# Three buffers for the queries' parts, one bank apart, square sums side by side, and the first block's keys in two halves, in a transformer block's opening stage

## The chip, the cores and the metric

The kernel runs on one core of one Trainium2 chip, as one launch. Its time is the device time of one execution in microseconds (us). A core has a matrix engine (TensorE, PE below), a vector engine (VectorE, DVE), an activation engine (ScalarE, ACT), a general engine (GpSimd, POOL), a sequencer that mostly issues DMAs (SyncE, SP), and 16 DMA engines between the device memory and the on-chip memory. Each engine has a queue of its own and works it off in order; waits between engines go by semaphores. Products of PE land in PSUM, which has eight banks of 128 rows by 512 fp32 values.

## The reference

One pre-norm transformer block: attention with 32 query heads of 16 and one shared key and value head, then a gated feed-forward part. Everything is fp32; S = 2048 tokens, D = 512, F = 1792.

```python
q = (layernorm(x) @ wq).reshape(B, S, 32, 16).transpose(0, 2, 1, 3)
k, v = layernorm(x) @ wk, layernorm(x) @ wv
p = softmax(einsum("bhqd,bkd->bhqk", q, k) * 16 ** -0.5)
h = x + einsum("bhqk,bkd->bhqd", p, v).transpose(0, 2, 1, 3).reshape(B, S, 512) @ wo
out = h + (gelu(layernorm(h) @ w_gate) * (layernorm(h) @ w_up)) @ w_down
```

## The kernel before, in words

The tokens are cut into four blocks of 512 (b = 0 to 3), a block into four tiles of 128 (t = 0 to 15 over all blocks), D into four chunks of 128 (c or d). An fp32 product is made of three products of fp32r parts, high x high, high x low and low x high; every operand is split by a cast (`hi`) and a subtraction (`lo`).

**The opening (`prologue`).** For every tile t the program loads x, takes its statistics on DVE and POOL, normalizes it on ACT (`xn`), turns it on PE (`pt`, four transposes into one PSUM bank), and splits it into `xT_hi` (ACT) and `xT_lo` (DVE). Turn t issues the work of several tiles: PE gets the transposes of tile t, then one chunk of the previous block's keys (`project_k`, tile `pk`, three products of 512 tokens), then one chunk of the first queries (`project_q`, tile `pq`). `idle` is a bank for transposes whose result nobody reads; they stand between the first turns to keep PE running. `wk_rep` repeats the key's 16 columns, so that one product gives several copies of k and, in spare rows, v. The keys' square sums (`norm_k`, tile `pkn`, weights `ones`) give the largest square norm `k2m`.

**Queries (`project_q`).** A query chunk (b, c) is 128 rows, that is eight heads. Its product `pq` is cast to `qh`, and `ql` is what is left; both come from pools of two buffers (tags `qh` and `ql`). For three chunks, `HURRY = ((0, 3), (1, 0), (1, 1))`, `pq` is first copied to SBUF (`pq_raw`: by ACT for block 0, by DVE for block 1), so that its bank is free early. `qs` is the square of `qh` in bf16. SP writes `qh`, `ql` and `qh` again to `q_d` in device memory, from where a group of four heads is loaded as `qg` for the scores; a buffer of `qh` or `ql` is free again when these writes have landed. When the four chunks of a block are done, a product with the 0/1 matrix `sel` sums the squares of each head's 16 rows (`pqn`, 32 rows for 32 heads; the four chunks add up in the same rows, each with its own 32 columns of `sel`). DVE copies it to `qn` and takes the maximum over the tokens (`q2`); POOL works out two numbers per head in four small steps (`mm`, from `q2` and `k2m`), DVE makes `m` from them, a bound on the scores that goes to `q_d` as one more row of the query. In block 0 chunk 0 goes first (`q_first`, urgent) with its own `pqn`, `mm` and `m`, so that the first scores can start; chunks 1 to 3 follow (`q_rest`).

**Attention (`run`).** Scores `s` (PE) go through ACT's exponential to `p`, five buffers; `weigh` multiplies `p` with v into `acc` (one bank, four groups of 32 rows). A list of moves written by hand (`OPENING`, `PERIOD`) weaves scores (s), sums (v) and pieces of later blocks' queries (p) through the first block, which ends near 312 us of the span; the order of PE, ACT, POOL, and there also of DVE and SP, is the order in which the program issues. All through the first block POOL splits the weights of the feed-forward part and writes them back (`part_weights`); the four steps of `mm` stand between in its queue. `evacuate` copies a finished `acc` to `oT` on DVE. Later blocks weave the feed-forward products into the attention.

In the opening PSUM's eight banks are one pool, from which `psum1` takes the next free one. `check_bound` writes the product of the largest `q2` and `k2m` to `b_d`, from which a flag is made that a safe path hangs on.

Of the kernel before, what the change touches and what calls it, by code (L numbers as in the profile page):

```python
# [19 lines left out]
P = 128  # L20
# [8 lines left out]
FIRST_Q = 1  # L29

HURRY = ((0, 3), (1, 0), (1, 1))

OPENING = "ssspssps"

# [23 lines left out]
def kernel(  # L58
# [12 lines left out]
    nc = tc.nc  # L71
# [35 lines left out]
    nc.vector.memset(power[:, 0:1], -0.5)  # L107
    nc.vector.memset(power[:, 1:2], 0.5)

    q2 = const.tile([H, NB + 1], F32, name="q2")  # L110
# [47 lines left out]
    def run(outer, first):  # L158
# [25 lines left out]
        if first:  # L184
            eb = early.enter_context(tc.tile_pool(name="early", bufs=1))

            xT = {
                b: [eb.tile([P, DC, T], F32R, name=f"xT_{w}_{b}") for w in ("hi", "lo")]
                for b in range(1, NB)
            }  # L190
            wq_hi = [eb.tile([P, DC, P], F32R, name=f"wq_hi_{c}") for c in range(DC)]
            wq_lo = [eb.tile([P, DC, P], F32R, name=f"wq_lo_{c}") for c in range(DC)]
            sel = eb.tile([P, DC, H], BF16, name="sel")
            k2m = eb.tile([H, T // 32 + 1], F32, name="k2m")[:, :1]


        def project_q(b, cs, eng, col):
            tsl = slice(b * T, (b + 1) * T)
            xT_hi, xT_lo = xT[b]
            urgent = b == 0 and cs[0] == 0  # L200
            qss = []
            for c in cs:
                pq = psum1(f"pq_{b}_{c}")
                n = 0
                for d in range(DC):
                    for wt, xt in ((wq_hi, xT_hi), (wq_hi, xT_lo), (wq_lo, xT_hi)):
                        nc.tensor.matmul(  # L207
                            pq, wt[c][:, d, :], xt[:, d, :],
                            start=(n == 0), stop=(n == 3 * DC - 1),
                        )  # L210
                        n += 1
                    if urgent or d < DC - 1:
                        yield 3

                raw = None
                if (b, c) in HURRY:
                    raw = eb.tile([P, T], F32, tag="vT", bufs=3, name=f"pq_raw_{b}_{c}")
                    if b == 0:
                        nc.scalar.activation(raw, pq, AF.Copy)
                    else:  # L220
                        nc.vector.tensor_copy(raw, pq)
# [12 lines left out]
                qss.append(qs)  # L234
                for r0, part in ((0, qh), (DH, ql), (2 * DH, qh)):
                    nc.sync.dma_start(
                        q_d[c * HC : (c + 1) * HC, r0 : r0 + DH, tsl].bitcast(F32),
                        part.bitcast(F32),
                    )
                if raw is None or b == 0:  # L240
                    yield 4 if b > 0 and c == DC - 1 else 3

            pn = psum1(f"pqn_{b}_{cs[0]}")[:H, :]
            for i, c in enumerate(cs):
                nc.tensor.matmul(
                    pn, sel[:, c, :], qss[i], start=(i == 0), stop=(i == len(cs) - 1)
                )
            qn = eb.tile([H, T], F32, tag="qn", bufs=1, name=f"qn_{b}_{cs[0]}")
            nc.vector.tensor_copy(qn, pn)
            nc.vector.tensor_reduce(q2[:, col : col + 1], qn, axis=AX.X, op=ALU.max)  # L250
            if urgent:
                yield 2
            mm = eb.tile([H, 3], F32, tag="mm", bufs=2, name=f"mm_{b}_{cs[0]}")
            nc.gpsimd.tensor_scalar(
                mm[:, 0:1], q2[:, col : col + 1], k2m, 1e-30, op0=ALU.mult, op1=ALU.add
            )
            nc.gpsimd.tensor_tensor(mm[:, 1:2], mm[:, 0:1], power[:H, 0:1], op=ALU.pow)
# [3 lines left out]
            nc.gpsimd.tensor_scalar(  # L261
                mm[:, 1:2], mm[:, 1:2], k2m, 0.5, op0=ALU.mult, op1=ALU.mult
            )
            m = eb.tile([H, T], F32R, tag="m", bufs=2, name=f"m_{b}_{cs[0]}")
# [7 lines left out]
            nc.vector.tensor_scalar(m, qn, mm[:, 1:2], mm[:, 2:3], op0=ALU.mult, op1=ALU.add)  # L272
            hs = slice(cs[0] * HC, (cs[-1] + 1) * HC)
            nc.sync.dma_start(q_d[hs, 3 * DH, tsl].bitcast(F32), m[hs].bitcast(F32))
            yield 0

        ms = {}
# [897 lines left out]
    def prologue(psum1, xT, wq_hi, wq_lo, sel, k2m, q_first, q_rest, advance, first_q, first_bound, eb):  # L1175
        with ExitStack() as pro:
# [25 lines left out]
            def repeat_k():  # L1202
# [8 lines left out]
                )  # L1211


            nc.gpsimd.memset(sel, 1.0)
            nc.gpsimd.affine_select(
                out=sel, in_=sel, compare_op=ALU.is_ge, fill=0.0, base=0,
                pattern=[[P, DC], [-DH, H]], channel_multiplier=1,
            )
            nc.gpsimd.affine_select(
                out=sel, in_=sel, compare_op=ALU.is_ge, fill=0.0, base=DH - 1,  # L1220
                pattern=[[-P, DC], [DH, H]], channel_multiplier=-1,
            )

            bias = sb.tile([P, 1], F32, name="bias")
# [5 lines left out]
            ones = sb.tile([DH, H], BF16, name="ones")  # L1230
            nc.vector.memset(ones, 1.0)
            k2 = sb.tile([H, NB], F32, name="k2")
            nc.vector.memset(v_sb, 1.0)

            zero = sb.tile([H, S], F32R, name="zero")
# [31 lines left out]
                    nc.vector.tensor_tensor, lo, pt, hi.bitcast(F32), op=ALU.subtract  # L1267
                )

            def project_k(b, c):  # L1270
                xT_hi, xT_lo = xT[b]
                if c == 0:
                    pks[b] = psum1(f"pk_{b}")
                for n, (wt, xt) in enumerate(((wk_hi, xT_hi), (wk_hi, xT_lo), (wk_lo, xT_hi))):
                    nc.tensor.matmul(  # L1275
                        pks[b], wt[:, c, :], xt[:, c, :],
                        start=(c == 0 and n == 0), stop=(c == DC - 1 and n == 2),
                    )

# [3 lines left out]
                return ks  # L1283

            def norm_k(b, ks):
                pn = psum1(f"pkn_{b}")[:H, :]
                nc.tensor.matmul(pn, ones, ks, start=True, stop=True)
                return pn

# [52 lines left out]
            for t in range(NT):  # L1342
# [86 lines left out]
    b_d = dram.tile([1, H], F32, name="b_d")  # L1429

    def check_bound(sb, k2m):
        q2m = sb.tile([H, 1], F32, name="q2m")
        nc.vector.tensor_reduce(q2m, q2, axis=AX.X, op=ALU.max)
        nc.vector.tensor_tensor(q2m, q2m, k2m, op=ALU.mult)
        nc.sync.dma_start(b_d.rearrange("o h -> h o"), q2m)

    def bound_flag(step):
        if step == 0:
# [74 lines left out]
```

## Time and profile before

| | us |
|---|---|
| median of 3 runs (lowest to highest) | 1410.09 (1409.43 to 1411.04) |
| the profiled execution | 1410.79 |
| its span, first to last instruction | 1409.1 |
| PE busy | 1390.7 (99%) |
| ACT busy | 1034.0 (73%) |
| DVE busy | 629.8 (45%) |
| POOL busy | 231.5 (16%) |

All times of the profile count from the span's start. A busy PE is one with a matmul in flight; matmuls overlap, so a row of several has a total, and the distance between starts is the price of one. A matmul on fp32 values that are not fp32r stands as two instructions. The opening lasts about 47 us, the first block of attention until about 312 us, and the last block's feed-forward part begins near 1200 us.

### The profile page before, as it was taken

The page shows a single profiled execution, that of the slowest core. Times are in us where ns is not written, and L with a number is a line of the kernel's source. Part 1 is how long each engine was busy: PE and PEld are TensorE (multiplying, and loading weights), DVE is VectorE, ACT ScalarE, POOL GpSimd, SP SyncE. Part 2 cuts the span into 40 slices and gives each one's busy share as a digit, 9 for nine tenths or more (in the row PEclk, how much of TensorE's full clock was granted, in tenths as well). Part 3 has the DMA queues.
Part 4 walks back from the last instruction along what each step waited for, and adds up shares of the span by engine and source line. Part 5 has one row for each costly group of instructions (what it writes and reads, how often), then busy time and mean ns, then how long its engine had stood idle before and what let it go on. Part 6 is the DMA issues. An engine that isn't in the chain of part 4 may idle for free.

```text
span 1409.1 us, 25259 instructions
## 1 busy us (share of the span) xinstructions
PE 1390.7 (99%) x10435; PEld 760.2 (54%) x10435; DVE 629.8 (45%) x1022; ACT 1034.0 (73%) x1155; POOL 231.5 (16%) x335
## 2 busy tenths in 40 slices
PE   9999999999999999999999999999999999999998
PEld 7433333325455555555555555545555555558886
DVE  7311231214364454454354453435264453546665
ACT  7699999997877777777777777787778777762000
POOL 7575777731000000000000000000000000011000
PEclk9999999999999999999999999999999999999999
DMA  4565776745222333311432333310433332233552
GB/s 161 159 189 177 231 235 217 240 144 189 69 91 83 117 106 113 102 65 57 156 104 87 119 116 102 103 65 28 149 102 102 117 102 101 92 120 114 193 204 96
DMA packets 66707, 180.32 MB, mean 128 GB/s; under 512 B 9596, under 2 KB 9596, under 8 KB 66552
## 3 DMA queue, kind: packets, MB, share of 16 engines
q1 hardware_dynamic: 55120, 143.15, 30.7%
q0 software_dynamic: 10208, 35.26, 7.6%
q8 instruction: 84, 1.38, 0.4%
q10 hardware_dynamic: 1256, 0.20, 0.1%
q14 instruction: 39, 0.32, 0.1%
HBM read 130.87 MB, written 47.45 MB: 127 GB/s over the span
## 4 chain that ended last, share of the span: by engine, by line
PE 95%; ACT 2%; DMA 1%; DVE 1%; issue 1%; POOL 0%; SPq 0%; ACTq 0%; DVEq 0%
PE acc L362 33%; PE s L354 20%; PE pu L781 9%; PE pg L781 8%; PE pd L781 8%; PE pq L207 3%; PE pd L811 3%; PE pg L811 3%; PE pu L811 3%; PE pp L781 2%; ACT p L358 1%; PE pk L1275 1%; PE pp L883 1%; PE pd_rest L823 1%; DMA x<-in_A_x_dram 0%
## 5 line engine op out<-in xcount | busy, mean ns | idle before, releaser
L358 ACT ACTIVATE p<-s 128x1024 f32<-128x1024 f32 x1024 | 960.0, 1037 | 233.3 <-PE s L354 230.5
L362 PE MATMUL acc<-p,v_sb 128*32 128x512 f32 x4096 | 491.6, 600 | 0.0
L354 PE MATMUL s<-qg,kaug 50*128 50x512 f32 x1984 | 387.6, 426 | 4.1 <-ACT p L358 4.1
L354 PEld LDWEIGHTS s<-qg,kaug 50*128 50x128 f32 x1984 | 169.5, 184 | 282.5 <-ACT p L358 123.6
L362 PEld LDWEIGHTS acc<-p,v_sb 128*32 128x32 f32 x4096 | 108.9, 109 | 232.8 <-issue 219.9
L781 PE MATMUL pg<-x2h,w 64*128 64x512 f32 x672 | 175.2, 392 | 0.0
L781 PE MATMUL pu<-x2h,w 64*128 64x512 f32 x672 | 174.0, 392 | 0.0
L781 PE MATMUL pd<-w,gh 64*128 64x512 f32 x624 | 124.9, 393 | 1.4 <-DVE h L711 1.4
L711 DVE TENSOR_TENSOR h<-h,pd 128x512 f32<-128x512 f32 x80 | 54.4, 687 | 148.5 <-PE pd L781 148.5
L137 POOL TENSOR_SCALAR rstd<-mv 128x1 f32<-128x1 f32 x16 | 3.5, 221 | 674.0 <-DVE mv L135 673.8
L781 PEld LDWEIGHTS pg<-x2h,w 64*128 64x128 f32 x672 | 95.5, 186 | 11.3
L781 PEld LDWEIGHTS pu<-x2h,w 64*128 64x128 f32 x672 | 95.2, 186 | 11.5
L781 PE MATMUL pg<-x2l,w 64*128 64x512 f32 x336 | 100.1, 392 | 0.0
L781 PE MATMUL pu<-x2l,w 64*128 64x512 f32 x336 | 99.6, 392 | 0.0
L781 PEld LDWEIGHTS pd<-w,gh 64*128 64x128 f32 x624 | 69.6, 186 | 12.5 <-DVE h L711 2.7
L939 ACT ACTIVATE ga<-ga 128x512 f32<-128x512 f32 x14 | 8.8, 632 | 88.5 <-DVE ga L936 88.5
L781 PE MATMUL pd<-w,gl 64*128 64x512 f32 x312 | 72.7, 392 | 0.0
L375 DVE COPY oT<-acc 128x512 f32<-128x512 f32 x32 | 22.1, 690 | 112.0 <-PE acc L362 111.9
L648 DVE TENSOR_TENSOR g<-g,pg 128x512 f32<-128x512 f32 x42 | 28.8, 685 | 90.8 <-PE pg L781 90.8
L398 DVE RECIPROCAL oc<-oc 128x128 f32<-128x128 f32 x64 | 56.6, 922 | 20.2 <-DMA oc<-acc_d 16.4
L644 DVE COPY g<-pg 128x512 f32<-128x512 f32 x42 | 29.1, 692 | 72.1 <-PE pg L781 72.1
L648 DVE TENSOR_TENSOR u<-u,pu 128x512 f32<-128x512 f32 x42 | 28.8, 686 | 68.7 <-PE pu L781 68.7
(258 smaller groups left out, 1481.6 us busy)
## 6 DMA issues: line engine op xcount, KB each, us to landing
w<-w_d SPq DMA_DIRECT2D x126, 512.0 KB
w<-w_d SPq DMA_DIRECT2D x21, 1024.0 KB
qg<-q_d SPq DMA_DIRECT2D x62, 200.0 KB
q_d<-qh SPq DMA_DIRECT2D x32, 256.0 KB
acc_d<-oT SPq DMA_DIRECT2D x31, 256.0 KB
oc<-acc_d SPq DMA_DIRECT2D x124, 64.0 KB
w_d<-w_0b POOLq DMA_DIRECT2D x14, 512.0 KB, 5.0
w_d<-w_1b POOLq DMA_DIRECT2D x14, 512.0 KB, 3.3
```

The lines of the kernel that those rows point to most:

```text
L207: nc.tensor.matmul(pq, wt[c][:, d, :], xt[:, d, :], start=(n == 0), stop=(n == 3 * DC - 1),)
L354: nc.tensor.matmul(s[:, a, :], kaug[rows, kc * P : (kc + 1) * P], qg[rows, u, :], start=True, stop=True,)
L358: nc.scalar.activation(p[:, 2 * u : 2 * u + 2, :], s, AF.Exp, scale=SCALE)
L362: nc.tensor.matmul(acc[32 * j : 32 * j + 32, :], v_sb[:, kc, :], p[:, j, :], start=(kc == 0), stop=(kc == KC - 1), skip_group_check=True,)
L375: nc.vector.tensor_copy(oT, acc)
L398: nc.vector.reciprocal(oc[:, 1, sl], oc[:, 1, sl])
L644: nc.vector.tensor_copy(half, bank)
L648: nc.vector.tensor_tensor(half, half, bank, op=ALU.add)
L711: nc.vector.tensor_tensor(hs[b, t], hs[b, t], bank, op=ALU.add)
L781: nc.tensor.matmul(bank, lhsT[r], rhs[r], start=(k == 0), stop=(k == n - 1), skip_group_check=True,)
L811: nc.tensor.matmul(bank, lhsT, rhs, start=(i == 0), stop=(i == len(ts) - 1))
L823: nc.tensor.matmul(bank, lhsT, rhs, start=(i == 0), stop=(i == len(ts) - 1))
```

## The change

- `qh` and `ql` have three buffers each.
- `idle`, `pq_0_0` and `pq_0_3` share one bank of their own (`APART`, tag `apart`); all other tiles of the opening take turns in the seven that are left.
- `sel` has one set of 32 columns, eight heads in rows 0 to 7 of 32. Each chunk's square sum goes to its own 32 rows of `pqn`, so the four products of a block write side by side instead of adding up. `qn`, `mm`, `m`, `q2`, `k2`, `k2m` have up to 128 rows accordingly, `ones` has 128 columns, `m` has one buffer, and its rows are written to `q_d` by one DMA per chunk; `b_d` is filled by four.
- Block 0's keys are made in two halves of 256 tokens: the first half, all four chunks, in the turn of tile 4, the second in the turns of tiles 5 and 6, two chunks each. In all blocks high x high is followed by `wk_lo` x high and then `wk_hi` x low.

```diff
+APART = "idle", "pq_0_0", "pq_0_3"
...
         def psum1(name):
+            if name in APART:
+                return ps.tile([P, T], F32, tag="apart", bufs=1, name=name)
...
-                qh = eb.tile([P, T], F32R, tag="qh", bufs=2, name=f"qh_{b}_{c}")
-                ql = eb.tile([P, T], F32R, tag="ql", bufs=2, name=f"ql_{b}_{c}")
+                qh = eb.tile([P, T], F32R, tag="qh", bufs=3, name=f"qh_{b}_{c}")
+                ql = eb.tile([P, T], F32R, tag="ql", bufs=3, name=f"ql_{b}_{c}")
...
-            pn = psum1(f"pqn_{b}_{cs[0]}")[:H, :]
-            for i, c in enumerate(cs):
+            rows = slice(0, 32 * len(cs))
+            pn = psum1(f"pqn_{b}_{cs[0]}")[rows]
+            for i in range(len(cs)):
                 nc.tensor.matmul(
-                    pn, sel[:, c, :], qss[i], start=(i == 0), stop=(i == len(cs) - 1)
-                )
+                    pn[32 * i : 32 * i + 32, :], sel, qss[i], start=True, stop=True,
+                    skip_group_check=True,
+                )
...
-            hs = slice(cs[0] * HC, (cs[-1] + 1) * HC)
-            nc.sync.dma_start(q_d[hs, 3 * DH, tsl].bitcast(F32), m[hs].bitcast(F32))
+            for i, c in enumerate(cs):
+                nc.sync.dma_start(
+                    q_d[c * HC : (c + 1) * HC, 3 * DH, tsl].bitcast(F32),
+                    m[32 * i : 32 * i + HC].bitcast(F32),
+                )
...
-            width = 8
+            width = 7
...
-            def project_k(b, c):
+            def project_k(b, c, sl=slice(0, T)):
...
-                for n, (wt, xt) in enumerate(((wk_hi, xT_hi), (wk_hi, xT_lo), (wk_lo, xT_hi))):
+                for n, (wt, xt) in enumerate(((wk_hi, xT_hi), (wk_lo, xT_hi), (wk_hi, xT_lo))):
                     nc.tensor.matmul(
-                        pks[b], wt[:, c, :], xt[:, c, :],
+                        pks[b][:, sl], wt[:, c, :], xt[:, c, sl],
...
+            K_HALVES = {0: (0, range(DC)), 1: (1, range(2)), 2: (1, range(2, DC))}
...
-                    if 0 <= step < DC:
+                    if b == 0 and step in K_HALVES:
+                        half, cs = K_HALVES[step]
+                        for c in cs:
+                            project_k(0, c, slice(half * T // 2, (half + 1) * T // 2))
+                    elif b > 0 and 0 <= step < DC:
                         project_k(b, step)
```

PE's queue in the turn of tile 4, before (the first number behind a name is its buffer's; `pk_360` is block 0's keys, `pt_374` is tile 5):

```order
L1332 MATMUL idle<-ident 128x128 x3
L1275 MATMUL pk_360<-xT_hi_113,wk_hi 128x512
L1275 MATMUL pk_360<-xT_lo_114,wk_hi 128x512
L1275 MATMUL pk_360<-xT_hi_113,wk_lo 128x512
L1261 MATMUL pt_374<-ident,xn_336 128x128 x4
```

And now (`pk_361` is block 0's keys):

```order
L1343 MATMUL idle<-ident 128x128 x3
L1285 MATMUL pk_361<-xT_hi_113,wk_hi 128x256
L1285 MATMUL pk_361<-xT_hi_113,wk_lo 128x256
L1285 MATMUL pk_361<-xT_lo_114,wk_hi 128x256
L1285 MATMUL pk_361<-xT_hi_113,wk_hi 128x256
```

The three products of 256 tokens stand there four times, twelve in all, ahead of tile 5's transposes; the product with `xT_lo` has moved from second to third.

PE's queue in the turn of tile 7, before (`pt_425` is tile 7, `pt_449` tile 8, `pq_0_385` the first queries):

```order
L1261 MATMUL pt_425<-ident,xn_380 128x128 x4
L1275 MATMUL pk_360<-xT_hi_113,wk_hi 128x512
L1275 MATMUL pk_360<-xT_lo_114,wk_hi 128x512
L1275 MATMUL pk_360<-xT_hi_113,wk_lo 128x512
L207 MATMUL pq_0_385<-xT_hi_113,wq_hi_94 128x512
L207 MATMUL pq_0_385<-xT_lo_114,wq_hi_94 128x512
L207 MATMUL pq_0_385<-xT_hi_113,wq_lo_98 128x512
L1261 MATMUL pt_449<-ident,xn_405 128x128 x4
```

And now (`pt_441` and `pt_462` are tiles 7 and 8):

```order
L1271 MATMUL pt_441<-ident,xn_390 128x128 x4
L211 MATMUL pq_0_398<-xT_hi_113,wq_hi_94 128x512
L211 MATMUL pq_0_398<-xT_lo_114,wq_hi_94 128x512
L211 MATMUL pq_0_398<-xT_hi_113,wq_lo_98 128x512
L1271 MATMUL pt_462<-ident,xn_418 128x128 x4
```

The keys' three products are gone from this turn.

PE's queue where the first scores start, with the semaphores that each row waits for, before (`s_0_781` and `s_1_785` are the first two score tiles):

```order
L207 MATMUL pq_3_746<-xT_hi_113,wq_lo_101 128x512
L354 MATMUL s_0_781<-qg_first,kaug 128x512 [waits DMAHW1_49,DMAHW6_49,DVE_49,Activation_49]
L354 MATMUL s_0_781<-qg_first,kaug 128x512 [waits DMAHW7_49,DMAHW2_49,DMAHW0_49]
L354 MATMUL s_1_785<-qg_first,kaug 128x512 [waits DMAHW3_49]
L354 MATMUL s_1_785<-qg_first,kaug 128x512 [waits DMAHW2_49]
```

And now (`s_0_794` and `s_1_798` are the same two):

```order
L211 MATMUL pq_3_759<-xT_hi_113,wq_lo_101 128x512
L363 MATMUL s_0_794<-qg_first,kaug 128x512 [waits DMAHW1_49,DMAHW6_49,DVE_49,Activation_49]
L363 MATMUL s_0_794<-qg_first,kaug 128x512 [waits DMAHW7_49,DMAHW2_49,DMAHW0_49]
L363 MATMUL s_1_798<-qg_first,kaug 128x512 [waits DMAHW3_49]
L363 MATMUL s_1_798<-qg_first,kaug 128x512 [waits DMAHW2_49]
```

Nothing has moved here: the first score product waits for DVE and ACT as before. DVE's, ACT's and SP's other instructions stand in the same order as before; only widths differ, and `m`'s writes are three or four in a row.

More of the change, by code (lines that the diff above doesn't have):

```diff
@@ L108 @@
     nc.vector.memset(power[:, 1:2], 0.5)
-    q2 = const.tile([H, NB + 1], F32, name="q2")
+    q2 = const.tile([P, NB + 1], F32, name="q2")
     flag = const.tile([1, 1], I32, name="flag")
@@ L192, in run @@
             wq_lo = [eb.tile([P, DC, P], F32R, name=f"wq_lo_{c}") for c in range(DC)]
-            sel = eb.tile([P, DC, H], BF16, name="sel")
-            k2m = eb.tile([H, T // 32 + 1], F32, name="k2m")[:, :1]
+            sel = eb.tile([P, DC * H], BF16, name="sel")[:, :H]
+            k2m = eb.tile([P, T // 32 + 1], F32, name="k2m")[:, :1]
         def project_q(b, cs, eng, col):
@@ L241, in project_q @@
                     yield 4 if b > 0 and c == DC - 1 else 3
-            pn = psum1(f"pqn_{b}_{cs[0]}")[:H, :]
-            for i, c in enumerate(cs):
+            rows = slice(0, 32 * len(cs))
+            pn = psum1(f"pqn_{b}_{cs[0]}")[rows]
+            for i in range(len(cs)):
                 nc.tensor.matmul(
-                    pn, sel[:, c, :], qss[i], start=(i == 0), stop=(i == len(cs) - 1)
-                )
-            qn = eb.tile([H, T], F32, tag="qn", bufs=1, name=f"qn_{b}_{cs[0]}")
+                    pn[32 * i : 32 * i + 32, :], sel, qss[i], start=True, stop=True,
+                    skip_group_check=True,
+                )
+            qn = eb.tile([P, T], F32, tag="qn", bufs=1, name=f"qn_{b}_{cs[0]}")[rows]
+            top = q2[rows, col : col + 1]
             nc.vector.tensor_copy(qn, pn)
-            nc.vector.tensor_reduce(q2[:, col : col + 1], qn, axis=AX.X, op=ALU.max)
+            nc.vector.tensor_reduce(top, qn, axis=AX.X, op=ALU.max)
             if urgent:
                 yield 2
-            mm = eb.tile([H, 3], F32, tag="mm", bufs=2, name=f"mm_{b}_{cs[0]}")
-            nc.gpsimd.tensor_scalar(
-                mm[:, 0:1], q2[:, col : col + 1], k2m, 1e-30, op0=ALU.mult, op1=ALU.add
-            )
-            nc.gpsimd.tensor_tensor(mm[:, 1:2], mm[:, 0:1], power[:H, 0:1], op=ALU.pow)
+            mm = eb.tile([P, 3], F32, tag="mm", bufs=2, name=f"mm_{b}_{cs[0]}")[rows]
+            km = k2m[rows]
+            nc.gpsimd.tensor_scalar(mm[:, 0:1], top, km, 1e-30, op0=ALU.mult, op1=ALU.add)
+            nc.gpsimd.tensor_tensor(mm[:, 1:2], mm[:, 0:1], power[rows, 0:1], op=ALU.pow)
             nc.gpsimd.tensor_scalar(
@@ L261, in project_q @@
             nc.gpsimd.tensor_scalar(
-                mm[:, 1:2], mm[:, 1:2], k2m, 0.5, op0=ALU.mult, op1=ALU.mult
+                mm[:, 1:2], mm[:, 1:2], km, 0.5, op0=ALU.mult, op1=ALU.mult
             )
-            m = eb.tile([H, T], F32R, tag="m", bufs=2, name=f"m_{b}_{cs[0]}")
+            m = eb.tile([P, T], F32R, tag="m", bufs=1, name=f"m_{b}_{cs[0]}")[rows]
             if urgent:
@@ L1211, in repeat_k @@
                 )
+            nc.gpsimd.memset(q2, 0.0)
             nc.gpsimd.memset(sel, 1.0)
@@ L1229, in prologue @@
                 nc.scalar.dma_start(bias[r0 + 3 * DH : r0 + KR, :], neg)
-            ones = sb.tile([DH, H], BF16, name="ones")
+            ones = sb.tile([DH, P], BF16, name="ones")
             nc.vector.memset(ones, 1.0)
-            k2 = sb.tile([H, NB], F32, name="k2")
+            k2 = sb.tile([P, NB], F32, name="k2")
             nc.vector.memset(v_sb, 1.0)
@@ L1431, in check_bound @@
     def check_bound(sb, k2m):
-        q2m = sb.tile([H, 1], F32, name="q2m")
+        q2m = sb.tile([P, 1], F32, name="q2m")
         nc.vector.tensor_reduce(q2m, q2, axis=AX.X, op=ALU.max)
         nc.vector.tensor_tensor(q2m, q2m, k2m, op=ALU.mult)
-        nc.sync.dma_start(b_d.rearrange("o h -> h o"), q2m)
+        for i in range(DC):
+            nc.sync.dma_start(
+                b_d[:, i * HC : (i + 1) * HC].rearrange("o h -> h o"),
+                q2m[32 * i : 32 * i + HC],
+            )
     def bound_flag(step):
```

8 lines of the change are left out of this document (4 added, 4 removed).

## The prediction

> **What bounds the kernel now.** I read the page first, then the table by stage, the waits of TensorE (PE), the chain of waits and the timeline of the first 62 us. The stage table (columns: stretch, its length, busy time of PE, PE weight loads, VectorE (DVE), ScalarE (ACT), GpSimd (POOL), granted PE clock, DMA share, GB/s) shows one broken place near the start:
>
> ```profile
> 42.00:52.60 10.60, 9.81 (x50) 6.84 (x48) 2.63 (x8) 6.69 (x9) 8.08 (x7) 1.00 0.48 129
> 52.60:55.10 2.50, 0.00 (x0) 0.00 (x0) 2.32 (x4) 1.02 (x2) 0.00 (x0) 0.91 0.52 202
> 55.10:62.00 6.90, 6.86 (x29) 1.97 (x28) 3.52 (x6) 2.85 (x3) 2.66 (x6) 0.54 0.60 197
> 62.00:125.00 63.00, 63.00 (x436) 23.20 (x432) 9.69 (x12) 61.67 (x66) 37.73 (x44) 1.00 0.58 183
> ```
>
> Between 52.6 and 55.1 PE runs nothing; in the 6.9 us after, its clock is 0.54. Behind 62 us ACT is all but full (61.67 of 63.00), and all later work keeps its order, so what the start gains, the end gains, unless something with a pace of its own holds it. Three of PE's waits in the whole run (sum, times, longest) lie in the start:
>
> ```profile
> PE pqn L245 <- DVE pq_raw L221: 2.6, 1, 2.6
> PE s L354 <- ACT pq_raw L219: 0.7, 1, 0.7
> PE pk L1275 <- DVE xT_lo L1349: 0.7, 1, 0.7
> ```
>
> What the 2.6 us hang on, first in the chain of waits (start, us, what), then in the timeline (start, us, idle before it in brackets):
>
> ```profile
> 46.51 6.11 DMA q_d<-qh
> ```
>
> ```profile
> 47.92 5.70 ACT L358 ACTIVATE p<-s 128x1024 f32<-128x1024 f32 x6 [0.70 <-PE s L354]
> 51.74 0.39 PE L207 MATMUL pq<-xT_hi,wq_lo 128*128 128x512 f32 x1
> 52.73 0.43 DVE L127 CAST qh<-pq_raw 128x512 fp32r<-128x512 f32 x1 [6.05 <-ACT p L358]
> 54.41 0.69 DVE L221 COPY pq_raw<-pq 128x512 f32<-128x512 f32 x1
> 55.14 1.44 PE L245 MATMUL pqn<-qs,sel 128*32 128x512 bf16 x3 [2.59 <-DVE pq_raw L221]
> 56.51 1.65 PE L354 MATMUL s<-qg_first,kaug 50*128 50x512 f32 x6
> 57.35 2.85 ACT L358 ACTIVATE p<-s 128x1024 f32<-128x1024 f32 x3 [3.72 <-PE s L354]
> 58.09 3.58 PE L362 MATMUL acc<-p,v_sb 128*32 128x512 f32 x16
> 62.14 14.19 ACT L358 ACTIVATE p<-s 128x1024 f32<-128x1024 f32 x15 [1.93 <-PE s L354]
> ```
>
> DVE's `qh` for (0, 3) starts 0.1 us after a write of `qh` lands (46.51 + 6.11 = 52.62). With two buffers it takes the one of (0, 1), which SyncE (SP) has just sent off. Behind it on DVE stand `ql`, `qs` and the copy of (1, 0), and PE holds the square sums and the next scores for that copy. The price is ACT's idle time: 3.72 + 1.93 us.
>
> **Third buffer (term A).** (0, 3) now takes the buffer of (0, 0), whose writes SP sent off from 33.60; (0, 2) took that buffer at 44.29 today and waited for PE alone:
>
> ```profile
> 33.60 1.34 SPq L236 DMA_DIRECT2D q_d<-qh  x2
> 44.29 0.60 ACT L125 ACTIVATE qh<-pq 128x512 fp32r<-128x512 f32 x1 [1.38 <-PE pq L207]
> ```
>
> So its cast can start when ACT's copy ends, at 47.92 - 0.70 = 47.22. Cast, `ql` and `qs` take 54.41 - 52.73 = 1.7 us today and would be done by 49; at twice that price still before 51. PE ends the product of (1, 0) at 51.74 + 0.39 = 52.13, so DVE's copy runs 52.15 to 52.84. That copy is what is late next: the square sums start at 52.85, not 55.14, and PE's pause shrinks from 2.59 to about 0.4 us. PE's wait of 0.7 us for `pq_raw` left the clock at 1.00 in the first stage row; I take it that 0.4 does too. At full clock the rows read:
>
> ```profile
> 205.45 1.03 PE L245 MATMUL pqn<-qs,sel 128*32 128x512 bf16 x4
> 206.40 0.97 PE L354 MATMUL s<-qg,kaug 50*128 50x512 f32 x6
> 207.30 1.92 PE L362 MATMUL acc<-p,v_sb 128*32 128x512 f32 x16
> ```
>
> Side by side, three sums take about 0.4 us (term B), so scores start at 53.25; ACT follows 0.55 later (206.40 to ACT's 206.95 below), at 53.8; six score products (0.9) and the sixteen rows of `acc` (1.9) end at 56.05, and ACT, busy with three exponentials until 53.8 + 2.85 = 56.65, need not wait. What stood at 62.14 stands at 56.65: **-5.5 us**. Bounds: -3.0 if the clock falls all the same (rival 1), -5.9 if nothing is left of the pause.
>
> **Square sums side by side (term B).** Three more times four sums stand in PE's row, 0.95 us from the first to the scores behind (205.45 to 206.40), each time with ACT idle there; two of them:
>
> ```profile
> 206.95 23.62 ACT L358 ACTIVATE p<-s 128x1024 f32<-128x1024 f32 x25 [0.97 <-PE s L354]
> 286.55 5.61 ACT L358 ACTIVATE p<-s 128x1024 f32<-128x1024 f32 x6 [0.56 <-PE s L354]
> ```
>
> The nearest row is `acc`, also 32 columns wide and written to four groups of 32 rows: 16 in 1.92 us, 0.12 each. Four sums would then take 0.46, 0.5 less, and ACT has 0.56 or more to give back: 3 x 0.5 = **-1.5 us**. Bounds: 0 (still one behind the other, 0.24 each) to -2.2 (one for all, 0.23).
>
> The Trainium skill's page "TensorE: Matmul & The Clock Gate" (Part 3, Measured speedup vs the span model) gives 2.38 times for three column tiles and 3.07 times for four row tiles. By an estimate from it the four would take 0.95 / 3.07 = 0.31 us and the term would be -1.9. No run here shows it yet.
>
> DVE's copies, maxima and `m` have up to 128 rows now at the same 512 columns; a copy of 128x512 costs 0.69 (54.41), and DVE idles before and after each. POOL and SP:
>
> ```profile
> L137 POOL TENSOR_SCALAR rstd<-mv 128x1 f32<-128x1 f32 x16 | 3.5, 221 | 674.0 <-DVE mv L135 673.8
> 126.79 0.26 POOL L254 TENSOR_SCALAR mm<-q,k2m 32x1 f32<-32x1 f32 x1 [11.62 <-ACT p L358]
> 301.93 0.34 SPq L274 DMA_DIRECT2D q_d<-m  x1
> ```
>
> A step of one column takes 0.22 on POOL with 128 rows and 0.26 with 32: no change. SP issues three or four small writes of `m` for one, 1 us more, ahead of writes of `acc_d` or loads of `oc`, and four of `b_d` at the last, so 2 us there. The scores and `acc` that PE and ACT run meanwhile hide them; without that cover the last costs up to 2 us.
>
> **First keys in halves (term C).**
>
> ```profile
> 13.14 0.47 PE L1275 MATMUL pk<-xT_hi,wk_hi 128*128 128x512 f32 x1
> 14.27 0.50 PE L1275 MATMUL pk<-xT_lo,wk_hi 128*128 128x512 f32 x1 [0.66 <-DVE xT_lo L1349]
> 14.27 0.19 PEld L1275 LDWEIGHTS pk<-xT_lo,wk_hi 128*128 128x128 f32 x1 [0.97 <-DVE xT_lo L1349]
> 14.61 0.39 PE L1275 MATMUL pk<-xT_hi,wk_lo 128*128 128x512 f32 x1
> 14.84 0.60 PE L1261 MATMUL pt<-ident,xn 128*128 128x128 f32 x4
> 17.07 0.82 ACT L1255 ACTIVATE xn<-x,shift,rstd 128x512 f32<-128x512 f32 x1 [1.00 <-DMA x<-in_A_x_dram]
> 20.41 0.68 DVE L1349 TENSOR_TENSOR xT_lo<-pt,xT_hi 128x512 fp32r<-128x512 f32 x1
> 21.14 0.50 PE L1275 MATMUL pk<-xT_lo,wk_hi 128*128 128x512 f32 x1
> 21.71 0.39 PE L207 MATMUL pq<-xT_hi,wq_hi 128*128 128x512 f32 x1
> ```
>
> A product of 512 tokens takes 0.23 (14.61 to 14.84); I price one of 256 at half, 0.12. The twelve of the first half need only tiles 0 and 1 and fill the wait: 13.14 + 0.2 + 12 x 0.12 = 14.8, where tile 5 is turned today. The next two turns cost the same, the one of tile 7 loses its three products, 0.8 us. But PE can't keep this: block 1's keys need tile 7's `xT_lo`, ready at 20.41 + 0.68 = 21.09 behind ACT's row that waited for `x`, whatever PE does. As third instead of second, that product starts at 21.1 and PE goes on at 21.4, not 21.71. Two later block starts stand alike and gain a little by the new order: **-0.5 us** together. Bounds: -0.9, and +0.9 if each of the twelve costs its weight load's whole 0.19 (PEld).
>
> **Bank apart (term D): 0.** The first score product keeps its wait for ACT's and DVE's last readers (0.7 us above); the order shows the same list. The seven other banks add no wait that ends late: gain at most 0.6.
>
> Sum: 5.5 + 1.5 + 0.5 = 7.5. The profiled execution took 1410.79 (span 1409.1 and 1.7 around it): 1403.3. The median of the runs is 0.7 lower, so I forecast **1402.6 us**. Less than 0.2% (2.8 us) can't be told from no change.
>
> **Rivals.**
>
> 1. *The clock falls all the same.* Then sums start at 52.85 and take 3 x 0.22 (`acc`: 3.58 / 16 in the slow stretch) instead of 1.37, and everything behind keeps its slow price: term A is -3.0. Time 1410.1 - 3.0 - 1.5 - 0.5 = 1405.1. Against it: the clock was 1.00 until the pause. The Trainium skill's page "TensorE: Matmul & The Clock Gate" (Part 1) has the clock halve only after an idle window of about 3.4 us that runs free of the program; by that rule a pause of 2.59 us need not be the cause, and the slow stretch could stay. The 0.54 right behind the pause speaks for the pause.
>
> 2. *The sums still run in turn*: A loses 0.5, B is 0: 1404.6.
>
> 3. *The cast waits as before* (the change doesn't do what it says; the third buffer isn't free by 47 us): only B and C are left, 1408.1. Against it speaks the row at 44.29.
>
> 4. *GpSimd's splitting of weights holds.* POOL falls behind in the first block (timeline; below it the longest group of POOL's own waits from 128 to 312 us, with its sum, times and longest):
>
> ```profile
> 301.36 0.53 DVE L272 TENSOR_SCALAR m<-qn,mm 32x512 fp32r<-32x512 f32 x1 [13.92 <-POOL mm L261]
> 303.04 0.69 DVE L375 COPY oT<-acc 128x512 f32<-128x512 f32 x1 [0.89 <-PE acc L362]
> 305.18 1.92 PE L362 MATMUL acc<-p,v_sb 128*32 128x512 f32 x16
> ```
>
> ```profile
> POOL w_1b L127 <- DMA w_1r<-in_B_w_up_dram: 19.9, 8, 5.5
> ```
>
> `m` at 301.36 waits for POOL, `oT` stands behind it on DVE with 0.89 us to spare, and PE needs the bank it empties 1.45 us after that. If POOL keeps its time, 2.3 us of all gains survive: 1407.8. For the forecast: POOL waited 11.6 us for `q2` at 126.79, so its long run starts there 6.5 us earlier, and 6.5 + 0.89 + 1.45 covers 7.5. The slower side is this mechanism's too: its waits for its loads (19.9 us in its longest group) keep their size only as long as traffic does. If that group grows by 70% (13.9) because the main work now moves the same bytes in less time, `m` is 13.9 - 6.5 = 7.4 later than today, 5.1 beyond the slack of 2.3: 1415.2. It makes the kernel slower than today from a growth of 8.8 us on.
>
> **Chances.** Forecast with its bounds 0.74, rival 1 0.08, rival 2 0.08, rival 3 0.02, rival 4 held 0.05, grown 0.03. The range takes in the forecast's bounds and rivals 1 and 2: the upper ends of A, B and C give 1410.1 - 5.9 - 2.2 - 0.9 = 1401.1, rival 1 with C at +0.6 gives 1406.2; I take 1400.9 to 1406.2. Faster by over 0.2%: 0.74 + 0.16 = 0.90; within: 0.07 (rivals 3, 4 held); slower: 0.03.
>
> **What would show it.** Right: no wait of PE over 0.7 us for DVE's copy; clock 1.00 from 47 to 62; the scores behind the first sums at 53 and ACT's row without 3.72 and 1.93; sums of four within 0.5 us; tile 8 turned at 19.5 and the first scores at 46.7. Wrong: a clock under 0.9 before 62 (rival 1), sums 0.24 apart (2), a cast that starts after 50 (3), `oT` near 300 right behind a late `m` (4), products of 256 spaced by 0.19 (C).

## The result and the profile after

The changed kernel takes 1403.32 us (median of 5 runs, 1403.08 to 1404.24) against 1410.09 of the kernel before (1409.43 to 1411.33 in 5 runs beside it). The ratio is 0.9953, with a 95% interval of 0.994 to 0.9966. Forecast were 1402.6, in a range of 1400.9 to 1406.2. The profiled execution took 1403.18 (span 1401.5); that of before 1410.79 (span 1409.1).

The stage table of the changed kernel, with the same stretches and columns as before:

```profile
42.00:52.60 10.60, 9.82 (x50) 6.87 (x48) 7.26 (x12) 6.68 (x8) 8.49 (x7) 1.00 0.46 128
52.60:55.10 2.50, 2.12 (x19) 0.91 (x22) 1.69 (x3) 2.27 (x4) 0.11 (x1) 1.00 0.52 203
55.10:62.00 6.90, 6.90 (x52) 2.82 (x48) 2.17 (x4) 6.79 (x8) 2.57 (x6) 1.00 0.65 202
```

The stretch in which PE ran nothing now holds 2.12 us of work, the clock is 1.00 where it was 0.91 and 0.54, and PE issues 52 products between 55.1 and 62 where it issued 29. PE's waits up to 62 us (sum, times, longest), apart from 1.5 us for `ident` at the very start, as before:

```profile
PE pt L1271 <- ACT xn L1265: 1.2, 4, 0.4
PE s L363 <- ACT pq_raw L223: 0.7, 1, 0.7
PE pqn L250 <- DVE pq_raw L225: 0.4, 1, 0.4
```

The wait for DVE's copy fell from 2.6 to 0.4, that for ACT's copy stayed at 0.7, that for `xT_lo` (0.7) is gone, and four waits for `xn` (1.2 in all) stand where one of 0.4 was. The timeline around the first square sums:

```profile
47.26 0.84 DVE L129 CAST qh<-pq_raw 128x512 fp32r<-128x512 f32 x1 [0.57 <-ACT pq_raw L223]
48.14 1.66 DVE L130 TENSOR_TENSOR ql<-pq_raw,qh 128x512 fp32r<-128x512 f32 x1
49.72 1.77 DVE L235 TENSOR_TENSOR qs<-qh 128x512 bf16<-128x512 f32 x1
52.23 0.69 DVE L225 COPY pq_raw<-pq 128x512 f32<-128x512 f32 x1 [0.74 <-PE pq L211]
52.98 0.40 PE L250 MATMUL pqn<-qs,sel 128*32 128x512 bf16 x3 [0.42 <-DVE pq_raw L225]
53.31 0.97 PE L363 MATMUL s<-qg_first,kaug 50*128 50x512 f32 x6
53.85 16.93 ACT L367 ACTIVATE p<-s 128x1024 f32<-128x1024 f32 x18 [0.23 <-PE s L363]
```

The cast of (0, 3) starts at 47.26, where it started at 52.73. Its three steps take 4.2 us together, where they took 1.7 before; that is almost two and a half times as much, more than the double price that the prediction allowed for, and they end at 51.5, still before PE ends (1, 0). ACT waits 0.23 us where it waited 3.72 and 1.93.

How the gain grows is read from ACT's rows. The same exponential stands in the timeline of before at

```profile
76.54 19.89 ACT L358 ACTIVATE p<-s 128x1024 f32<-128x1024 f32 x21 [0.22 <-PE s L354]
138.53 30.27 ACT L358 ACTIVATE p<-s 128x1024 f32<-128x1024 f32 x32 [0.19 <-PE s L354]
230.76 30.27 ACT L358 ACTIVATE p<-s 128x1024 f32<-128x1024 f32 x32 [0.19 <-PE s L354]
292.38 15.07 ACT L358 ACTIVATE p<-s 128x1024 f32<-128x1024 f32 x16 [0.22 <-PE s L354]
```

and in that of the changed kernel at

```profile
70.99 30.29 ACT L367 ACTIVATE p<-s 128x1024 f32<-128x1024 f32 x32 [0.21 <-PE s L363]
132.35 30.27 ACT L367 ACTIVATE p<-s 128x1024 f32<-128x1024 f32 x32 [0.19 <-PE s L363]
223.96 30.27 ACT L367 ACTIVATE p<-s 128x1024 f32<-128x1024 f32 x32 [0.19 <-PE s L363]
284.96 15.07 ACT L367 ACTIVATE p<-s 128x1024 f32<-128x1024 f32 x16 [0.23 <-PE s L363]
```

The differences are 5.55, 6.18, 6.80 and 7.42: one step of 5.55 at the start and three of 0.62 to 0.63, one at each later place with four square sums. The span is 7.6 shorter, so the rest keeps it. By the medians the gain is 6.8. At one of those places the sums and the scores behind them are now

```profile
118.60 0.40 PE L250 MATMUL pqn<-qs,sel 128*32 128x512 bf16 x4
118.93 0.73 PE L363 MATMUL s<-qg,kaug 50*128 50x512 f32 x4
```

0.33 us apart, against 0.95. Rival 4's place, where `m` waits for POOL and `oT` stands behind `m` on DVE:

```profile
293.96 0.26 POOL L262 TENSOR_SCALAR mm<-q,k2m 128x1 f32<-128x1 f32 x1
295.64 0.55 DVE L278 TENSOR_SCALAR m<-qn,mm 128x512 fp32r<-128x512 f32 x1 [15.57 <-POOL mm L267]
296.36 0.69 DVE L384 COPY oT<-acc 128x512 f32<-128x512 f32 x1
297.77 1.92 PE L371 MATMUL acc<-p,v_sb 128*32 128x512 f32 x16
```

POOL came forward by 5.75 (299.71 to 293.96) and PE by 7.41 (305.18 to 297.77). `oT` ends at 297.05, 0.72 ahead of the sums that need its bank. POOL doesn't hold the work in this execution; 0.72 us are left. That is little beside POOL's own spread: in two further traces of the changed kernel (the last group below) the same first step of `mm` starts at 293.17 and 291.66.

The opening gained nothing: the first scores start at 47.28, as before (47.27). Rows of the changed kernel:

```profile
12.14 0.82 ACT L1265 ACTIVATE xn<-x,shift,rstd 128x512 f32<-128x512 f32 x1 [0.20 <-POOL shift L1258]
13.95 0.28 PE L1285 MATMUL pk<-xT_hi,wk_lo 128*128 128x256 f32 x1
14.07 0.28 PE L1285 MATMUL pk<-xT_lo,wk_hi 128*128 128x256 f32 x1
47.28 1.02 PE L363 MATMUL s<-qg_first,kaug 50*128 50x512 f32 x6 [0.75 <-ACT pq_raw L223]
```

Products of 256 tokens stand 0.12 apart, as forecast. But `xn` of tile 4 starts at 12.14, and in the kernel before it starts at

```profile
11.53 0.82 ACT L1255 ACTIVATE xn<-x,shift,rstd 128x512 f32<-128x512 f32 x1
```

so the halves begin 0.6 us later than the keys did. Tile 8 is still turned 0.24 us earlier (20.08 against 20.32), but tile 7's `xT_lo`, for which block 1's keys wait, ends at 21.54 and not at 21.09.

### The profile page after: what moved, and what is told of

It is laid out like the page before. It is cut to its first block, busy times and chain, and to the rows that moved or that the text cites. A ratio compares the mean times of both kernels' runs of the same rounds, so it can differ in the third digit from the quotient of the medians.

```text
span 1401.5 us, 25298 instructions
## 1 busy us (share of the span) xinstructions
PE 1385.0 (99%) x10447; PEld 757.2 (54%) x10447; DVE 634.6 (45%) x1022; ACT 1033.9 (74%) x1155; POOL 232.3 (17%) x336
## 4 chain that ended last, share of the span: by engine, by line
PE 95%; ACT 2%; DVE 1%; issue 1%; DMA 0%; POOL 0%; SPq 0%; DVEq 0%; ACTq 0%
PE acc L371 33%; PE s L363 21%; PE pu L790 9%; PE pg L790 8%; PE pd L790 8%; PE pq L211 3%; PE pd L820 3%; PE pg L820 3%; PE pu L820 3%; PE pp L790 2%; ACT p L367 1%; PE pp L892 1%; PE pk L1285 1%; PE pd_rest L832 1%; PE pxt L616 0%
```

## Experiments

The theory: (A) the third buffer is worth 5.5 us, of which the pause of PE is a part and the slow clock behind it the rest; (B) the sums side by side are worth 1.5 to 1.9; (C) the keys in halves are worth 0.5; (D) the bank apart nothing; and POOL (rival 4) stands close behind. Runs of one group shared a chip. The changed kernel itself took 1403.18 on the chip of the third group; on those of the first and second the nearest kernels stand for it, the one without the bank apart (1403.43) and the one with three idle copies (1403.07).

**Undoing A.** `bufs=3` back to 2 for `qh` and `ql`.

```diff
-                qh = eb.tile([P, T], F32R, tag="qh", bufs=3, name=f"qh_{b}_{c}")
+                qh = eb.tile([P, T], F32R, tag="qh", bufs=2, name=f"qh_{b}_{c}")
```

> The changed kernel (1403.3) with two buffers of qh and ql again; everything else stays. If the third buffer carries the gain, the cast of (0, 3) waits for the write of (0, 1) again until about 52.7, PE pauses about 2.6 us ahead of the square sums, the clock falls to about 0.54 behind it, and the time is 5 to 5.5 us more: 1408.3 to 1408.8. If the pause and the slow stretch went for another reason (the sums side by side, the bank apart, the earlier keys), the clock stays at 1.00 and the time is within 1 us of 1403.3.

Measured: 1408.36 (1405.57 to 1413.22), ratio to before 0.9988 (0.9979 to 0.9997); 4.9 more than the kernel without a bank apart below, which stands for the full change in this group (1403.43). In its timeline:

```profile
54.93 0.61 PE L250 MATMUL pqn<-qs,sel 128*32 128x512 bf16 x3 [2.57 <-DVE pq_raw L225]
56.31 2.86 ACT L367 ACTIVATE p<-s 128x1024 f32<-128x1024 f32 x3 [2.88 <-PE s L363]
61.44 14.21 ACT L367 ACTIVATE p<-s 128x1024 f32<-128x1024 f32 x15 [2.28 <-PE s L363]
...
303.67 0.55 DVE L278 TENSOR_SCALAR m<-qn,mm 128x512 fp32r<-128x512 f32 x1 [18.70 <-POOL mm L267]
305.14 3.64 PE L371 MATMUL acc<-p,v_sb 128*32 128x512 f32 x16 [2.42 <-DVE oT L384]
309.62 1.94 ACT L367 ACTIVATE p<-s 128x1024 f32<-128x1024 f32 x2 [4.69 <-PE s L363]
```

The pause of 2.57 and ACT's two stalls are back: A is shown. The profiled execution was the longest of its eleven (1413.22), and its last three rows show why: rival 4 happened. `m` came late from POOL, `oT` behind it, PE paused 2.42 us and ran the next sums at half clock (3.64 for sixteen), and ACT lost 4.69.

**Undoing B.** The sums add up in the same 32 rows again, with the wide `sel` and one write of `m` for four.

```diff
-                    pn[32 * i : 32 * i + 32, :], sel, qss[i], start=True, stop=True,
-                    skip_group_check=True,
+                    pn, sel[:, c, :], qss[i], start=(i == 0), stop=(i == len(cs) - 1)
```

> The changed kernel with the square sums added up in the same 32 rows again, one after the other, and with one write of m for four. Forecast's step: 0.46 us for four sums side by side against 0.95, at three later places and once at the start (three sums), so about 2 us more: 1405.3. By the 0.33 us that the changed kernel's trace has for four, it is 0.62 at three places and 0.3 to 0.5 at the start: 2.2 to 2.4 more, 1405.6. If the sums' time is hidden behind ACT's work: within 0.5 of 1403.3.

Measured: 1405.36 (1404.86 to 1406.47), ratio 0.997 (0.996 to 0.9981); 1.9 more. But the trace shows that the size is not B's alone:

```profile
300.23 3.56 PE L367 MATMUL acc<-p,v_sb 128*32 128x512 f32 x16 [0.56 <-DVE oT L380]
304.33 13.86 ACT L363 ACTIVATE p<-s 128x1024 f32<-128x1024 f32 x15 [2.46 <-PE s L359]
```

In this execution POOL was late too: 0.56 us of waiting for `oT`, and 2.46 of ACT's time, since the clock fell. Up to there its rows of exponentials fall behind the changed kernel's by 0.40 at the first sums and by 0.56, 0.59 and 0.64 at the three later places, 1.8 in these three and 2.2 in all. That agrees with the three steps of 0.62 between the two traces above.

**Undoing C.** Keys of block 0 in one piece, old order of the products.

```diff
-                    if b == 0 and step in K_HALVES:
...
-                    elif b > 0 and 0 <= step < DC:
+                    if 0 <= step < DC:
                         project_k(b, step)
```

> The changed kernel with block 0's keys in one piece of 512 tokens and the old order of the three products. Forecast's step: 0.5 us more, 1403.8, with PE's wait of 0.7 us for xT_lo back. What the two traces suggest instead (first scores at 47.27 before and 47.28 after): no difference, the first scores still within 0.1 us of 47.3. If the halves cost by their weight loads and only the new order helps: 0.3 to 0.9 less.

Measured: 1403.97 (1403.38 to 1411.76), ratio 0.9969 (0.9959 to 0.9978); 0.5 more than without the bank apart. The one execution of 1411.76 among twelve has no trace, and its cause is open. In the timeline:

```profile
48.19 1.03 PE L363 MATMUL s<-qg_first,kaug 50*128 50x512 f32 x6 [0.75 <-ACT pq_raw L223]
```

With tile 4's `xn` at 12.23, as late as in the changed kernel (12.14), the first scores start 0.9 later. Counted from that `xn`, the first scores come 35.1 to 35.2 us later in the ten traces with halves and the old pool, and 35.7 (before) and 36.0 (this run) in the two without halves. So C is worth 0.5 to 0.9, and "no difference" was wrong: between before and after it was hidden by the later start.

What makes that start later is in part seen in the traces. POOL's fifth `rstd`, which leads to tile 4's `xn`, is in the changed kernel

```profile
10.31 0.77 POOL L1255 TENSOR_SCALAR rstd<-mv 128x1 f32<-128x1 f32 x1
```

It takes 0.71 to 0.77 in all twelve traces with the sums side by side; before and with the sums in turn it takes 0.21, and the step behind it 0.85 in place of 0.57. POOL's three steps for the tile thus take 1.8 us (1.7 in one trace) in place of 1.5. In each of the 14 traces DVE's `wk_lo` starts within 0.05 us of that `rstd`. The rest of the 0.6 differs from execution to execution: `xn` of tile 4 starts between 11.86 and 12.23 with the sums side by side, at 11.69 with the sums in turn and at 11.53 before. No run took this apart, so its cause stays open.

**Undoing D.**

```diff
-APART = "idle", "pq_0_0", "pq_0_3"
+APART = ()
-            width = 7
+            width = 8
```

> The changed kernel with eight banks in one ring and none apart. Forecast's step: nothing, within 0.5 us of 1403.3, and the first scores still wait about 0.7 us for ACT's copy pq_raw of (0, 3). If the bank apart is worth what it takes out of the ring: up to 0.6 more; if the seven banks left are too few: up to 0.6 less.

Measured: 1403.43 (1403.17 to 1403.49), ratio 0.9959 (0.9946 to 0.9971). Nothing, as forecast.

**A longer pause with three buffers.** Idle copies on DVE ahead of the copy of (1, 0), three and then five.

```diff
+                        if c == 0:
+                            for _ in range(3):
+                                spin = eb.tile([P, T], F32, tag="qn", bufs=1, name="spin")
+                                nc.vector.tensor_copy(spin, v_sb.rearrange("p k d -> p (k d)"))
                         nc.vector.tensor_copy(raw, pq)
```

> The changed kernel with three idle copies of 128x512 on DVE between qs of (0, 3) and the copy of (1, 0): PE's pause ahead of the first square sums grows from 0.4 to about 1.6 us with three buffers in place and nothing else moved. If a pause costs only its length: 1.2 us more, 1404.5, clock 1.00 behind it. If any pause of this length brings the clock down, as after 2.59 us before: about 0.54 for some 6 us and 3.5 to 4 us more, 1407.

> The same with five idle copies: a pause of about 2.8 us. If the pause is what brought the clock down in the kernel before: 0.54 behind it and 4.5 to 5.5 us more, 1408 to 1408.8. By the Trainium skill's page TensorE: Matmul & The Clock Gate (Part 1), which has the clock halve only after an idle window of about 3.4 us, the clock would stay at 1.00, and the time would be the pause alone: 2.4 more, 1405.7. If something else than the pause brought it down (the traffic of the writes of qh), the same 1405.7.

The copies took 0.45 each, so the pauses are shorter than expected. With three, in the timeline:

```profile
53.18 0.40 PE L254 MATMUL pqn<-qs,sel 128*32 128x512 bf16 x3 [0.87 <-DVE pq_raw L229]
```

Measured 1403.07 (1402.77 to 1404.77), ratio 0.9959 (0.9947 to 0.9972): a pause of 0.87 costs nothing that the times show (ACT waits 0.68 us there in place of 0.23), and the clock stays at 1.00. With five, timeline and table by stretch:

```profile
54.17 0.40 PE L254 MATMUL pqn<-qs,sel 128*32 128x512 bf16 x3 [1.76 <-DVE pq_raw L229]
```

```profile
51.25:54.70 3.45, 1.69 (x11) 0.82 (x11) 2.82 (x8) 2.22 (x3) 0.00 (x0) 1.00 0.53 199
54.70:58.15 3.45, 3.45 (x18) 1.03 (x20) 1.60 (x3) 2.85 (x3) 1.33 (x4) 0.51 0.57 215
```

Measured 1406.34 (1404.84 to 1407.43), ratio 0.9981 (0.9972 to 0.9991): 3.3 more than with three copies, for 0.89 us more of pause. The clock is halved for 3.45 us behind the pause. No write of `qh` was moved, so the pause alone does it. Not all of the 3.3 belongs to it: in the two traces ACT's row of 32 exponentials starts at 73.80 and at 71.19, 2.6 apart, and the one with five copies loses another 1.4 of ACT's time near 290, where the clock fell once more.

**Two buffers with the pause filled.** Twenty transposes that nobody reads, ahead of the first square sums.

```diff
+            if b == 0 and not urgent:
+                for _ in range(20):
+                    nc.tensor.transpose(acc[:, :P], ident, ident)
```

> The changed kernel with two buffers again, and 20 transposes whose result nobody reads (about 2.2 us) on PE ahead of the first square sums, where it otherwise pauses for 2.6 us. The square sums still wait for the same copy. If the gain of the third buffer is half the pause and half the slow clock behind it: clock 1.00 from 55 to 62, and 2.2 to 2.6 us more than the changed kernel, 1405.7, against 1408.4 without the transposes. If the slow clock comes from elsewhere or costs nothing: 1408.4 as without them.

```profile
52.51 2.40 PE L251 MATMUL acc<-ident 128*128 128x128 f32 x20
55.12 0.40 PE L253 MATMUL pqn<-qs,sel 128*32 128x512 bf16 x3 [0.21 <-DVE pq_raw L225]
55.98 14.21 ACT L370 ACTIVATE p<-s 128x1024 f32<-128x1024 f32 x15 [2.34 <-PE s L366]
```

Measured: 1405.2 (1404.39 to 1406.87), ratio 0.9977 (0.9968 to 0.9987). The scores are as late as with two buffers (ACT waits 2.34), but ACT's second stall is gone: 2.1 more than with three copies, where two buffers alone cost 4.9 on the other chip. So of A the lost time itself is 2.1 and the clock 2.8. The traces agree: from ACT's first exponential to its row of 32 behind the pause pass 23.05 us in the changed kernel, 25.21 here and 28.14 with two buffers alone, which makes 2.2 and 2.9.

**POOL made later.** Four idle powers ahead of block 3's `mm`.

```diff
+            if b == NB - 1:
+                for _ in range(4):
+                    spin = eb.tile([P, 3], F32, tag="mm", bufs=2, name=f"spin_{b}_{cs[0]}")
+                    nc.gpsimd.tensor_tensor(spin[:, 0:1], k2m, power[:, 0:1], op=ALU.pow)
```

> The changed kernel with four idle powers of 128x1 on POOL (0.67 us each, 2.7 in all) ahead of block 3's mm near 294 us. In the changed kernel's trace oT stands right behind m on DVE and ends at 297.05, and PE's sums that need its bank start at 297.77: a cover of 0.7. If that is all there is: PE waits about 2.0 us there and the time is 2.0 us more, 1405.3, or 4 more, 1407.3, if the pause brings the clock down as well (in the run with two buffers a pause of 2.42 us at this place was followed by sums at 0.23 each instead of 0.12). If POOL's queue has more room than it shows: 1403.3.

Measured: 1403.92 (1402.68 to 1404.16), ratio 0.9963 (0.9949 to 0.9977). Inconclusive: the powers took 2.12 in all, POOL had been 0.85 earlier by itself, and in the profiled execution the clock fell at 287.2 for another reason (next paragraph), so that PE came 1.15 later and `oT` was ready. That POOL can hold the work is shown by the two executions above, not by this run.

**The rest: a base, and a better version.** The first kernel is the changed one again. The second was meant to move block 3's `m` behind `oT`; its edit (one more `yield 2` ahead of `m`) left every engine's order as it was, so it is a further run of the changed kernel.

> The changed kernel once more, as the base for the three beside it: 1403.0 to 1403.6, first exponential at 47.6 to 48.0.

> The changed kernel with block 3's m one visit later, so that on DVE it stands behind the copy of acc to oT for which PE waits, and not ahead of it; POOL's four steps stay where they are. If POOL's lateness (rival 4) still costs the changed kernel something in some executions, those lose nothing here any more: oT ends about 1.5 us ahead of the sums that need its bank, and the highest times go, the lowest stay; the median is 0 to 0.5 us less. If POOL has no part in the changed kernel's time: no difference, highest times neither.

Measured: 1403.18 (1402.99 to 1403.38), ratio 0.9957 (0.9943 to 0.9971), and 1403.19 (1401.24 to 1403.44), the same ratio. Whether a later `m` takes away the long executions stays open. So does what made one execution of 1401.24. In the first one's profile the clock fell where it didn't in the profile above:

```profile
283.75:287.15 3.40, 2.26 (x18) 0.86 (x10) 0.00 (x0) 3.18 (x4) 2.45 (x3) 1.00 0.51 162
287.15:290.60 3.45, 3.45 (x18) 0.91 (x20) 0.00 (x0) 3.01 (x4) 1.91 (x2) 0.51 0.40 165
```

The third has the second's edit too, and opens the bank apart as a pool of its own, closed only once the scores' pool is open:

```diff
+            apart = held_apart.enter_context(
+                tc.tile_pool(name="ps_apart", bufs=1, space=PSUM)
+            )
             set_banks("ps_pro")
...
+        held_apart.close()
         set_banks("ps_first")
```

> As e10, and the bank of idle, pq_0_0 and pq_0_3 is a pool of its own that is closed only after the scores' pool is opened, so that the first two score tiles no longer wait for ACT's copy of (0, 3) (the list of semaphores loses ACT's). If that wait of 0.7 us is what delays ACT's first exponential: scores at 46.6 in place of 47.3, the exponentials 0.6 to 0.7 earlier and the time 0.6 to 0.7 less than e10, 1402.5. If it is a wait for something that ends as late (the row of m in the first query group): within 0.2 of e10.

```profile
46.19 1.31 PE L369 MATMUL s<-qg_first,kaug 50*128 50x512 f32 x6
53.07 16.93 ACT L373 ACTIVATE p<-s 128x1024 f32<-128x1024 f32 x18 [0.22 <-PE s L369]
```

Measured: 1402.74 (1402.16 to 1404.02), ratio 0.9955 (0.9941 to 0.997). PE's wait of 0.7 is gone. Against the base of this group, whose row of eighteen exponentials starts at

```profile
53.59 16.97 ACT L367 ACTIVATE p<-s 128x1024 f32<-128x1024 f32 x18 [0.22 <-PE s L363]
```

the same exponential is 0.52 earlier, and the median is 0.44 less. It is the fastest version of this study by its median, though the difference is less than the spread of its runs.

The fourth also puts one score tile ahead of the first square sums:

```diff
-            for move in OPENING + PERIOD * (PER // KC):
+            for move in OPENING + "sp" + PERIOD[2:] + PERIOD * (PER // KC - 1):
```

> As e11, and one score tile of the first period stands ahead of the first square sums and not behind them, so that PE has 0.33 us of work in the 0.4 us in which it waits for DVE's copy of (1, 0). If that pause is what leaves ACT idle for 0.23 us behind its first six exponentials: 0.2 less than e11, 1402.3. If ACT's idle time comes from the order of the scores and not from the pause: the same as e11.

Measured: 1403.04 (1402.39 to 1404.07), ratio 0.9955 (0.9941 to 0.9969). No gain: PE's wait for the copy fell from 0.42 to 0.19 us, but ACT's two waits around it stayed what they were in the third (0.29 and 0.23, against 0.28 and 0.22). So the part of the pause that was taken away cost nothing.

## Why the prediction was right, and where a size was off

- **Term A, -5.5:** measured 5.55 between the traces, 0.4 to 0.5 of it by the first three sums standing side by side, as reckoned. The steps hold one by one: the cast at 47.26 (47.22 forecast), the copy at 52.23 (52.15), the sums at 52.98 (52.85), ACT at 53.85 (53.8). Rivals 1, 2 and 3 are out. The split was not in the prediction: 2.1 lost time, 2.8 clock. The clock's part was not sure to be there: of the 22 executions of the kernel before beside the second group, the eight with a mean granted clock of 0.999 took 1406.9 to 1407.4, the fourteen with 0.997 or 0.998 took 1408.3 to 1411.0. The profile that the forecast rests on was one of the longer kind, as most were.
- **Term B, -1.5:** mis-sized. The row it was taken from (`acc`, 0.12 for each product) was the wrong neighbour: the four sums take 0.33, not 0.46, and the three places gave 1.87. The mechanism was right. The estimate from the Trainium skill's page "TensorE: Matmul & The Clock Gate" (Part 3, Measured speedup vs the span model), 0.31 and -1.9, was nearer.
- **Term C, -0.5:** the net of the two traces is 0, and undoing it costs 0.5 to 0.9. The mechanism and the price of 0.12 were right. The step that failed is "tile 8 turned at 19.5 and the first scores at 46.7": it took tile 4's `xn` for unmoved by the change, and that starts 0.6 later. Tile 8 was turned at 20.08, and tile 7's `xT_lo`, reckoned for 21.09 whatever PE does, ended at 21.54.
- **Term D, 0:** right. A bank apart within a pool that is closed ahead of the scores left their wait as it was (0.75); in a pool closed behind them it took the wait away. Whether the scores wait for the closing of the whole pool or for a bank that they take over isn't shown.
- **Rival 4:** its margin was narrower than forecast (0.72, against 6.5 + 0.89 + 1.45 - 7.5 = 1.3), because POOL came forward by 5.75, not 6.5: its long run started 6.13 earlier (126.79 to 120.66) and lost 0.4 on the way. It did not decide the median, but it struck in two profiled executions of the kernels with two buffers and with sums in turn. POOL's spread between traces of the changed kernel is 2.3 us, so it is in part luck that it stayed away from the changed kernel's profile.
- **The total:** 7.6 in the two profiles against 7.5 forecast. That it fits so well is luck: the terms' errors offset each other, B gave 0.4 more, C 0.5 less. By the medians the gain is 6.8, because the forecast took 0.7 off for the distance of the median from the profiled execution, and the changed kernel has no such distance (1403.32 against 1403.18).

## What to carry to other kernels

Price a pause of the matrix engine with the clock behind it: here 2.57 us of waiting cost 4.9, because the 6.83 us behind it ran at half speed, and filling the pause with work that nobody reads returned more than half of that. When work in front gets faster, look for the engine that has a pace of its own and read its distance in the new trace, since a cover of 0.7 us can be gone in the next execution.

## What the runs showed of the hardware

**The clock falls by windows.** In the kernel before, around the pause (table by stretch):

```profile
51.20:54.65 3.45, 1.36 (x7) 0.70 (x6) 1.88 (x4) 2.42 (x3) 0.00 (x0) 1.00 0.52 198
54.65:58.05 3.40, 2.91 (x9) 1.07 (x8) 1.79 (x3) 0.70 (x1) 0.00 (x0) 0.50 0.55 201
58.05:61.50 3.45, 3.45 (x18) 0.59 (x16) 1.73 (x4) 2.15 (x3) 2.52 (x6) 0.50 0.59 197
```

The traces keep the times at which the clock changed. In all 14 of them the stretches between two changes are whole numbers of 3.413 us: in the kernel before 47.79 us at full clock (14), 6.83 at half (2) and 1344.85 at full (394), in the base of the last group 279.89 (82), 3.41 (1) and 1109.33 (325). The first change to the full clock falls between 4.5 and 7.3 us of the span, so the windows lie differently in each execution. The 3.4 us ahead of each fall in the first 330 us held 1.1 to 2.1 us without work (3.45 less 1.36 here, 3.40 less 2.26 in the base of the last group), in several pieces or one; 0.87 was not enough in the run with three copies. Between 1.07 and 1.14 us it went both ways, four falls against five windows without one; each of the five windows with more brought a fall. Near the program's end three windows with 1.6 to 1.9 us brought no fall, so this share isn't the whole rule.

The same 1.1 us of waiting near 286 brought the clock down in one profile of the changed kernel (the base of the last group, above) and not in the first one. There a boundary of its windows lies between the two waits, and each window holds only a part (0.71 and 0.42 us):

```profile
282.65:286.06 3.41, 2.70 (x24) 0.78 (x19) 0.00 (x0) 3.18 (x5) 2.33 (x3) 1.00 0.72 217
286.06:289.48 3.42, 3.00 (x20) 1.04 (x24) 0.00 (x0) 3.42 (x4) 0.20 (x2) 1.00 0.50 195
```

This fits windows that run freely of the program, as the Trainium skill's page "TensorE: Matmul & The Clock Gate" (Part 1) has them, with a length of about 3.4 us. Its table lets the clock fall after an idle window; the traces show that a third of a window idle can be enough.

**DVE beside POOL.** Cast, `ql` and `qs` of (0, 3) took 0.84, 1.66 and 1.77 at 47 to 51, where POOL was at work on `kaug` (until 50.94), and 0.43, 0.69 and 0.68 in the kernel before, when POOL was idle. With two buffers again they take 0.43, 0.69 and 0.69, behind POOL's work as before.
